# Attention on full 128x128 matmuls, and doubles converted in six VectorE instructions

## The chip, the cores and the metric

One core of a Trainium2 chip runs the whole program. The metric is device time in microseconds (us) from one execution to the next; lower is better. TensorE does matmuls (PE in the rows, its weight loads PEld), VectorE is DVE, ScalarE is ACT, GpSimd is POOL, SyncE (SP) issues most DMAs.

## The reference

Three parts follow one another: attention with a compressive memory (32 heads of 576 queries and 64 dimensions), a mixture of 8 experts where each token takes one, and a dense FFN.

```python
scores = scale * q @ k.T                         # B, H, S, D = 4, 8, 576, 64
scores = where(causal, -1e9, scores)
a = softmax(scores)
local = a @ v
q_p = where(q > 0, q, exp(q) - 1) + 1
mem_out = (q_p @ M_prev) / (q_p @ z_prev + 1e-6)
x = g * mem_out + (1 - g) * local                # to 2304 tokens x 512
...
expert_idx = argmax(normalized(x) @ normalized(expert_emb).T / tau)
out[e] = gate * (relu(x[e] @ w1[e]) @ w2[e])     # 512 -> 1024 -> 512
...
h = x @ w_in                                     # 512 -> 2048 -> 512
return (h * clip(h + 3, 0, 6) / 6) @ w_out
```

The weights of the last part arrive as 64-bit floats' bit patterns (the doubles of the title) and are turned into 32-bit ones on the chip.

## The kernel before

**Attention** runs over 16 pairs of heads. A pair has nine score tiles of 128 queries: t = 0 to 3 of head 0 (y = 0), then t = 4, which holds the last 64 queries of both heads (q4, L212), then t = 0 to 3 of head 1. For each tile, `scores` (L250 on) issues the score matmuls with a mask added by one bf16 matmul (L274, L276), VectorE takes the maximum (L281) and ScalarE the exponential (L287); `turn` transposes the result (L297, L301) and ScalarE copies it to aT (L298, L302); `sumup` multiplies it with the values (L310); `finish` normalizes and adds the memory's part (L315 to L321). The loop runs scores five tiles ahead of `turn` (LA = 5) and `sumup` one behind; three PSUM tiles hold scores, two hold po.

A head has 64 dimensions, so a score matmul contracts over 64 rows. For pairs 1 to 15 the product is made in fp32r from split operands: kx holds the high part of k on the head's own 64 partitions and the low part on the other 64, so that one 128-row matmul of qx (the high part of q on both halves) gives high x (high + low) (L269); a second one, on 64 rows, adds ql, the low part of q (L270). Tile t = 0 of every head, and pair 0 wholly, use fp32 matmuls on 64 rows (L266). A fp32 matmul is two instructions in the trace, a fp32r one is one. The operands are made by `split_pair` (qs on ScalarE L209, kx L220 and L222, qx on VectorE L221, ql on GpSimd L223), nine tiles ahead of the pair's first `turn`, so four ahead of its first score tile; the loads are 18 ahead (`load_pair`).

`mem_pair` makes the memory's part (L228 to L248): five matmuls of 130 columns (L236), the last with a stationary operand of 64 columns. In `sumup`, t = 4 is done twice, once a head, with a stationary operand of 64 columns and, for the last keys, 64 rows (128*64 and 64*64 in the rows). `route_pair` and `route` choose experts; at a batch's end (4 pairs) GpSimd scatters token ids by indirect DMA (L399).

**The experts** run in slots of 256 or 128 tokens, eight steps a slot: weights are split into fp32r high (ScalarE, L726) and low (GpSimd or VectorE, L727), hidden layer in `l1` (L735 to L737), its result split into hh and hl (ScalarE L781, VectorE L782), and down projection (L793 to L795) two steps later, which needs hl. Beside it `piece` converts the dense weights, 32 pieces of 512 elements, by `to_f32`: seven VectorE instructions (L680 to L686) and one on GpSimd (L687).

**The dense FFN** runs last, in nine chunks of 256 tokens.

The order on each engine is a scheduler's: program order where data allow, with operations that are ready earlier moved ahead.

## Time and profile before

| | |
|---|---|
| time, median of 3 runs | 1119.07 us (1113.79 to 1120.48) |
| profiled execution | 1113.76 us, span 1112.1 us |
| mean granted TensorE clock | 0.946 |
| TensorE busy | 1039.5 us (93%), 7214 matmuls |
| VectorE, ScalarE, GpSimd busy | 59%, 43%, 35% |
| DMA | 116.90 MB, mean 105 GB/s |

The span runs from the first to the last instruction of the profiled execution. Matmuls are pipelined, so the time that one takes off the span is the distance from its start to the next one's start; the listed duration also holds what overlaps the neighbour. A row's stretch shows stages that the mean over the span hides.

### The profile page before, as it was taken

The numbers are of one execution on the slowest core, as the hardware profiler recorded it, in microseconds if no ns is written. First come the engines' busy times: TensorE is split into PE (matmuls) and PEld (weight loads), VectorE is DVE, ScalarE is ACT, GpSimd is POOL, SyncE is SP. The second block draws the span as 40 slices with busy tenths as digits, with TensorE's granted clock in tenths as the row PEclk, the third lists the DMA queues.
The fourth block names the chain that finished last, engine by engine and source line by source line (L and its number), as shares of the span: only waits on it lengthen the run. The fifth ranks groups of instructions, "written<-read, shape, count | busy, mean of one in ns | idle before, by whom it ended". The sixth has DMA issues, their size and how long they took to land. (4 is left out here: it accounts for less than half of the span.)

```text
span 1112.1 us, 19567 instructions
## 1 busy us (share of the span) xinstructions
PE 1039.5 (93%) x7214; PEld 924.5 (83%) x7214; DVE 651.5 (59%) x1548; ACT 479.6 (43%) x997; POOL 390.7 (35%) x320
## 2 busy tenths in 40 slices
PE   8999899999998888978888889999999999999996
PEld 6778678788778888978887888898989999999895
DVE  5777556645767868688788877732333333333332
ACT  5766445536554444244144425432333333333332
POOL 4444424333545557476376643540000000000000
PEclk9999769959999999899988989999999999999998
DMA  9443924633326965675676555002000000000000
GB/s 215 109 114 90 137 71 101 105 96 89 34 59 245 198 200 188 223 253 198 224 240 225 191 198 213 3 2 21 20 1 19 20 1 20 10 10 20 1 19 20
DMA packets 89655, 116.90 MB, mean 105 GB/s; under 512 B 54856, under 2 KB 59336, under 8 KB 89552
## 3 DMA queue, kind: packets, MB, share of 16 engines
q1 hardware_dynamic: 85072, 105.08, 35.1%
q0 software_dynamic: 4480, 10.51, 2.5%
q8 instruction: 58, 0.95, 0.4%
q14 instruction: 45, 0.37, 0.1%
HBM read 105.64 MB, written 9.91 MB: 104 GB/s over the span
## 5 line engine op out<-in xcount | busy, mean ns | idle before, releaser
L1007 DVE SCALAR_TENSOR_TENSOR t<-t,ph 128x256 f32<-128x256 f32 x144 | 60.5, 420 | 168.4 <-ACT t L1005 166.9
L737 PE MATMUL ph<-xl,hw 128*128 128x256 f32 x468 | 136.3, 291 | 7.9 <-DVE xl L746 7.9
L727 POOL TENSOR_TENSOR lw<-rw,hw 128x1024 fp32r<-128x1024 f32 x50 | 126.1, 2530 | 43.1 <-ACT hw L726 29.5
L977 POOL DMA_INDIRECT out<-ob,pmt x18 | 17.3, 960 | 341.9 <-DVE ob L1023 306.0
L1005 ACT ACTIVATE t<-ph,half 128x256 f32<-128x256 f32 x144 | 68.4, 475 | 159.8 <-PE ph L737 159.0
L736 PE MATMUL ph<-xh,lo 128*128 128x256 f32 x480 | 134.1, 279 | 0.0
L735 PE MATMUL ph<-xh,hw 128*128 128x256 f32 x448 | 131.6, 294 | 0.2 <-ACT xh L745 0.2
L310 PE MATMUL po<-vt,aT 128*128 128x65 f32 (+2 forms) x960 | 127.3, 268 | 4.0 <-ACT aT L298 2.5
L310 PEld LDWEIGHTS po<-vt,aT 128*128 128x128 f32 (+2 forms) x960 | 116.4, 187 | 13.5 <-issue 5.5
L795 PE MATMUL py<-hl,hw 128*128 128x256 f32 x288 | 88.3, 307 | 37.2 <-DVE hl L782 36.0
L726 ACT CAST hw<-rw 128x1024 fp32r<-128x1024 f32 x72 | 75.5, 1050 | 109.1 <-PE py L795 85.5
L281 DVE TENSOR_REDUCE nmx<-ps 128x1 f32<-128x256 f32 (+4 forms) x160 | 74.8, 477 | 68.8 <-PE ps L274 40.2
L298 ACT COPY aT<-ptr 128x128 f32<-128x128 f32 (+2 forms) x144 | 63.7, 445 | 103.0 <-PE ptr L297 97.8
L988 PE MATMUL po<-lo,gh 128*128 128x512 f32 x270 | 106.9, 396 | 0.0
L737 PEld LDWEIGHTS ph<-xl,hw 128*128 128x128 f32 x468 | 92.9, 198 | 9.3 <-DVE xl L746 9.3
L1011 DVE TENSOR_TENSOR gl<-t,gh 128x256 fp32r<-128x256 f32 x144 | 61.3, 425 | 64.7 <-ACT gh L1010 64.7
L736 PEld LDWEIGHTS ph<-xh,lo 128*128 128x128 f32 x480 | 90.5, 189 | 4.7
L736 PE MATMUL ph<-xh,lw 128*128 128x256 f32 x320 | 94.2, 294 | 0.0
L795 PEld LDWEIGHTS py<-hl,hw 128*128 128x128 f32 x288 | 59.6, 207 | 40.5 <-DVE hl L782 38.9
L1010 ACT CAST gh<-t 128x256 fp32r<-128x256 f32 x144 | 58.5, 406 | 77.2 <-DVE t L1007 77.2
L687 POOL TENSOR_TENSOR x<-f,u 128x512 int32<-128x512 int32 x32 | 56.8, 1775 | 98.9 <-DVE f L686 98.9
L735 PEld LDWEIGHTS ph<-xh,hw 128*128 128x128 f32 x448 | 89.6, 200 | 1.5 <-ACT xh L745 0.4
(299 smaller groups left out, 2772.0 us busy)
## 6 DMA issues: line engine op xcount, KB each, us to landing
rw<-in_wm SPq DMA_DIRECT2D x92, 512.0 KB, 3.9
raw<-in_w SPq DMA_DIRECT2D x32, 512.0 KB, 5.7
k<-in_kT SPq DMA_DIRECT2D x30, 256.0 KB, 5.0
q<-in_qT SPq DMA_DIRECT2D x30, 192.0 KB, 5.0
kp<-in_kT SPq DMA_DIRECT2D x16, 288.0 KB, 3.0
qp<-in_qT SPq DMA_DIRECT2D x16, 288.0 KB, 4.1
vt<-in_v SPq DMA_DIRECT2D x32, 128.0 KB, 4.9
xg<-xb SPq DMA_DIRECT2D x16, 256.0 KB, 5.3
```

The lines of the kernel that those rows point to most:

```text
L281: nc.vector.tensor_reduce(nmx[:, k:k + 1], ps, AX.X, ALU.max, negate=True)
L298: ev(aT[:, :nf].rearrange("p j r -> p (j r)"), ptr[:, :nf * P])
L310: nc.tensor.matmul(po[:r, t, :], aT[:kn, j, c:c + r], vt[:kn, y, j, :], start=(j == 0), stop=(j == t))
L726: st["copy"] = nc.scalar.copy(hi, raw)
L727: st["split"] = eng.tensor_tensor(lo, raw, hi.bitcast(F32), ALU.subtract)
L735: nc.tensor.matmul(ph, a, xh, start=(c == 0), stop=False)
L736: nc.tensor.matmul(ph, b, xh, start=False, stop=False)
L737: nc.tensor.matmul(ph, a, xl, start=False, stop=(c == 3))
L795: nc.tensor.matmul(o, a, hl, start=False, stop=(f == 7 and d % 2 == 1))
L988: nc.tensor.matmul(po[t], a, lo[:, 512:], start=False, stop=False)
L1005: nc.scalar.activation(t6, ph, AF.Relu, bias=half[:, :1], scale=1.0 / 6.0)
L1011: low = nc.vector.tensor_tensor(gl, gg, gh.bitcast(F32), ALU.subtract)
```

## The change

- `sumup` does t = 4 once for both heads: vt is laid out by key tile and then head, so that the values of both heads stand side by side and one full matmul gives 64 queries of either head times 130 columns; the diagonal blocks of the result are used. The last 64 keys lie on partitions 64 to 127 of vt behind 64 rows of zeros, and `turn` transposes the last 128 columns of a.
- `split_pair` loads and splits all 512 queries: q2 is scaled in place by ScalarE, qx is one copy, and ql one subtraction on all 128 partitions. t = 0 of pairs 1 to 15 uses the split operands too, and the ql matmul contracts over 128 rows, which adds low x low.
- `mem_pair` pads ph to five full tiles and copies the result out in two instructions instead of three.
- `finish` of head 0 runs after its fourth tile, and that of head 1 takes the last queries of both heads.
- `to_f32` masks small values by a float maximum instead of a compare and an and.

Pair 0's scores stay on 64 rows.

```diff
@@ -91,28 +91,29 @@
...
-    vt_b = [ac.tile([P, 2, NT, D + 1], F32, name=f"vt{i}", tag=f"vt{i}") for i in range(3)]
+    vt_b = [ac.tile([P, NT, 2, D + 1], F32, name=f"vt{i}", tag=f"vt{i}") for i in range(3)]
     for vt in vt_b:
         nc.vector.memset(vt[:, :, :, D:], 1.0)
+        nc.vector.memset(vt[:64, 4], 0.0)
...
-            q2 = p2.tile([P, 2, KW - P], F32, name="q2", tag="q2")
+            q2 = p2.tile([P, 2, KW], F32, name="q2", tag="q2")
...
-            nc.sync.dma_start(out=q2[o], in_=qflat[h, P:KW].rearrange("(y d) s -> d y s", y=2))
+            nc.sync.dma_start(out=q2[o], in_=qflat[h, :KW].rearrange("(y d) s -> d y s", y=2))
...
         for y in range(2):
-            nc.sync.dma_start(out=vt[:, y, :4, :D], in_=vi[y, :4 * P].rearrange("(c p) d -> p c d", p=P))
-        nc.sync.dma_start(out=vt[:64, :, 4, :D], in_=vi[:, 4 * P:].rearrange("y p d -> p y d"))
+            nc.sync.dma_start(out=vt[:, :4, y, :D], in_=vi[y, :4 * P].rearrange("(c p) d -> p c d", p=P))
+        nc.sync.dma_start(out=vt[64:, 4, :, :D], in_=vi[:, 4 * P:].rearrange("y p d -> p y d"))
@@ -194,51 +198,51 @@
...
-    rs_b = [ac.tile([P, NT], F32, name=f"rs{i}", tag=f"rs{i}") for i in range(2)]
+    rs_b = [ac.tile([P, 4 + i], F32, name=f"rs{i}", tag=f"rs{i}") for i in range(2)]
...
     def split_pair(i, ld):
         kp, qp, k2, q2, vt = ld
-        qs = p2.tile([P, KW], F32, name="qs", tag="qs")
         q4 = q4_b[i % 3]
-        nc.scalar.mul(qs, qp[:, :KW], 0.125)
+        if i == 0:
+            qs = ac.tile([P, KW], F32, name="qs", tag="qs")
+            nc.scalar.mul(qs, qp[:, :KW], 0.125)
+        else:
+            nc.scalar.mul(q2, q2, 0.125)
         for y in range(2):
             r = slice(64 * y, 64 * y + 64)
             nc.vector.tensor_scalar(q4[r, 64 * y:64 * y + 64], qp[r, KW:], 0.125, None, ALU.mult)
         if i == 0:
             return kp, qs, q4, None, None, None, vt
         kx = p2.tile([P, 2, KW], F32R, name="kx", tag="kx")
-        qx = p2.tile([P, 2, KW - P], F32R, name="qx", tag="qx")
-        ql = p2.tile([P, KW - P], F32R, name="ql", tag="ql")
+        qx = p2.tile([P, 2, KW], F32R, name="qx", tag="qx")
+        ql = p2.tile([P, 2, KW], F32R, name="ql", tag="ql")
+        nc.vector.tensor_copy(qx, q2)
         for y in range(2):
-            r, o = slice(64 * y, 64 * y + 64), slice(64 - 64 * y, P - 64 * y)
+            o = slice(64 - 64 * y, P - 64 * y)
             (nc.scalar.copy if y else nc.vector.tensor_copy)(kx[:, y], k2[:, y])
-            nc.vector.tensor_scalar(qx[:, y], q2[:, y], 0.125, None, ALU.mult)
             nc.gpsimd.tensor_tensor(kx[o, y], k2[o, y], kx[o, y].bitcast(F32), ALU.subtract)
-            nc.gpsimd.tensor_tensor(ql[r], qs[r, P:], qx[r, y].bitcast(F32), ALU.subtract)
-        return kp, qs, q4, kx, qx, ql, vt
+        nc.gpsimd.tensor_tensor(ql, q2, qx.bitcast(F32), ALU.subtract)
+        return kp, None, q4, kx, qx, ql, vt
...
-        ph = p2.tile([P, S], F32, name="ph", tag="ph")
-        nc.scalar.activation(ph, qp, AF.Relu)
...
+        ph = p2.tile([P, NT * P], F32, name="ph", tag="ph")
+        nc.scalar.activation(ph[:, :S], qp, AF.Relu)
+        yield
+        nc.vector.scalar_tensor_tensor(ph[:, :S], ex, 1.0, ph[:, :S], ALU.min, ALU.add)
+        nc.vector.tensor_copy(ph[:, S:], ph[:, 4 * P:S])
         for lo, hi in ((0, 3), (3, 5)):
             pm = ps_m.tile([P, 512], F32, name="pm", tag="pm")
             for t in range(lo, hi):
-                nc.tensor.matmul(pm[:RT[t], (t - lo) * W:(t - lo + 1) * W], ph[:, t * P:t * P + RT[t]],
-                                 mz[:, i, :], start=True, stop=True)
-            n = min(hi, 4) - lo
-            nc.scalar.copy(mem[:, lo:lo + n].rearrange("p t y d -> p (t y d)"), pm[:, :n * W])
-            if hi == 5:
-                nc.scalar.copy(mem[:64, 4].rearrange("p y d -> p (y d)"), pm[:64, n * W:(n + 1) * W])
+                nc.tensor.matmul(pm[:, (t - lo) * W:(t - lo + 1) * W], ph[:, t * P:(t + 1) * P], mz[:, i, :],
+                                 start=True, stop=True)
+            nc.scalar.copy(mem[:, lo:hi].rearrange("p t y d -> p (t y d)"), pm[:, :(hi - lo) * W])
@@ -262,12 +266,11 @@
...
-                if t == 0 or t < 4 and kx is None:
+                if t < 4 and kx is None:
                     nc.tensor.matmul(o, qs[r, c], kp[r, x0:x1], start=True, stop=False)
                 elif t < 4:
-                    c = slice((t - 1) * P, t * P)
                     nc.tensor.matmul(o, qx[:, y, c], kx[:, y, x0:x1], start=True, stop=False)
-                    nc.tensor.matmul(o, ql[r, c], kx[r, y, x0:x1], start=False, stop=False)
+                    nc.tensor.matmul(o, ql[:, y, c], kx[:, y, x0:x1], start=False, stop=False)
@@ -298,28 +301,38 @@
...
-            nc.tensor.transpose(pt2[:64, :P], a[:, 4 * P:], ident)
-            nc.scalar.copy(aT[:64, 4], pt2[:64, :P])
+            nc.tensor.transpose(pt2[:, :P], a[:, S - P:], ident)
+            nc.scalar.copy(aT[:, 4], pt2[:, :P])
         return aT
 
     def sumup(t, aT, vt, po, y):
-        r = RT[t]
-        c = 64 * y if t == 4 else 0
+
         for j in range(t + 1):
-            kn = RT[j]
-            nc.tensor.matmul(po[:r, t, :], aT[:kn, j, c:c + r], vt[:kn, y, j, :], start=(j == 0), stop=(j == t))
+            o, w = po[:, t * D1:(t + 1) * D1], vt[:, j, y, :]
+            if t == 4:
+                o, w = po[:, 4 * D1:], vt[:, j].rearrange("p y d -> p (y d)")
+            nc.tensor.matmul(o, aT[:, j, :], w, start=(j == 0), stop=(j == t))
...
     def finish(i, y, po, mem, xb):
         h = (2 * i + y) % H
         rs = rs_b[y]
-        nc.vector.tensor_scalar(rs[:, :4], po[:, :4, D], 1e-9, None, ALU.add)
-        nc.vector.tensor_scalar(rs[:64, 4:5], po[:64, 4, D:], 1e-9, None, ALU.add)
+        o = po[:, :4 * D1].rearrange("p (t d) -> p t d", d=D1)
+        nc.vector.tensor_scalar(rs[:, :4], o[:, :, D], 1e-9, None, ALU.add)
+        if y:
+            for z in range(2):
+                r, e = slice(64 * z, 64 * z + 64), (5 + z) * D1
+                nc.vector.tensor_scalar(rs[r, 4:5], po[r, e - 1:e], 1e-9, None, ALU.add)
         nc.vector.reciprocal(rs, rs)
-        nc.vector.tensor_scalar(rs, rs, omg[:, h:h + 1], None, ALU.mult)
-        for t in range(NT):
-            r = RT[t]
-            nc.vector.scalar_tensor_tensor(xb[:r, t, h * D:(h + 1) * D], po[:r, t, :D], rs[:r, t:t + 1],
-                                           mem[:r, t, y, :D], ALU.mult, ALU.add)
+        nc.vector.tensor_scalar(rs[:, :4], rs[:, :4], omg[:, h:h + 1], None, ALU.mult)
+        for t in range(4):
+            nc.vector.scalar_tensor_tensor(xb[:, t, h * D:(h + 1) * D], o[:, t, :D], rs[:, t:t + 1],
+                                           mem[:, t, y, :D], ALU.mult, ALU.add)
+        if y:
+            nc.vector.tensor_tensor(rs[:, 4:5], rs[:, 4:5], omg4[:, h // 2:h // 2 + 1], ALU.mult)
+            for z in range(2):
+                r, e = slice(64 * z, 64 * z + 64), (4 + z) * D1
+                nc.vector.scalar_tensor_tensor(xb[:64, 4, (h - 1 + z) * D:(h + z) * D], po[r, e:e + D],
+                                               rs[r, 4:5], mem[r, 4, z, :D], ALU.mult, ALU.add)
@@ -609,11 +622,9 @@
...
             if u == 0 or u == 4:
-                pos[j, u > 0] = ps_o.tile([P, NT, D + 1], F32, name="po", tag="po")
-            for yy in ((y,) if t < 4 else (0, 1)):
-                sumup(t, aTs[m], sp[j][-1], pos[j, yy], yy)
-            aTs.pop(m)
-            if u == 4 or u == 8:
+                pos[j, u > 0] = ps_o.tile([P, 6 * (D + 1)], F32, name="po", tag="po")
+            sumup(t, aTs.pop(m), sp[j][-1], pos[j, u >= 4], y)
+            if u == 3 or u == 8:
                 finish(j, y, pos.pop((j, y)), mem_b[j % 2], xb_b[bj % 2])
@@ -670,20 +681,19 @@
 
 def to_f32(nc, cv, src, dst, n):
...
-    m = cv.tile([P, n], I32, name="m", tag="m", bufs=1)
-    v.tensor_scalar(f, hi, 4, 1, ALU.logical_shift_left, ALU.logical_shift_right)
-    v.tensor_scalar(m, hi, 1, None, ALU.logical_shift_left)
+    v.tensor_scalar(f, hi, 1, 1, ALU.logical_shift_left, ALU.logical_shift_right)
+    v.tensor_scalar(f.bitcast(F32), f.bitcast(F32), 2.0 ** -15, None, ALU.max)
     v.tensor_scalar(u, lo, 28, 1, ALU.logical_shift_right, ALU.bitwise_and)
-    v.scalar_tensor_tensor(f, lo, 29, f, ALU.logical_shift_right, ALU.bitwise_xor)
-    v.tensor_scalar(m, m.bitcast(mybir.dt.uint32), float(897 << 21), -1.0, ALU.is_ge, ALU.mult)
-    v.scalar_tensor_tensor(f, f, 0x40000000, m, ALU.bitwise_xor, ALU.bitwise_and)
-    v.scalar_tensor_tensor(f, hi, -0x80000000, f, ALU.bitwise_and, ALU.bitwise_or)
+    v.tensor_scalar(f, f, 3, 0x3fffffff, ALU.logical_shift_left, ALU.bitwise_and)
+    v.scalar_tensor_tensor(f, lo, 29, f, ALU.logical_shift_right, ALU.bitwise_or)
+    v.scalar_tensor_tensor(f, hi, -0x40000000, f, ALU.bitwise_and, ALU.bitwise_or)
     return nc.gpsimd.tensor_tensor(dst, f, u, ALU.add)
```

## Rows read from the trace of the kernel before

**Rows 1.** Stretches: length, busy us (count) PE, PEld, DVE, ACT, POOL; granted clock, DMA.

```profile
15.00:125.00 110.00, 108.05 (x801) 84.74 (x799) 79.46 (x258) 71.43 (x168) 49.87 (x42) 1.00 0.57 111
125.00:156.00 31.00, 28.46 (x118) 21.86 (x119) 13.94 (x44) 10.88 (x27) 8.29 (x7) 0.51 0.57 131
217.00:248.00 31.00, 30.79 (x129) 24.39 (x130) 15.70 (x47) 12.36 (x30) 11.85 (x10) 0.51 0.42 100
352.00:695.00 343.00, 293.66 (x2287) 287.50 (x2286) 272.26 (x421) 136.24 (x219) 193.80 (x102) 0.94 0.66 214
```

**Rows 2.** The same columns, ahead of the second stretch at a lower clock.

```profile
214.70:217.60 2.90, 0.66 (x6) 0.47 (x6) 1.08 (x5) 1.03 (x3) 0.00 (x0) 1.00 0.75 45
```

**Rows 3.** The page's costliest groups: busy us, mean ns, idle us before, releaser.

```profile
L795 PE MATMUL py<-hl,hw 128*128 128x256 f32 x288 | 88.3, 307 | 37.2 <-DVE hl L782 36.0
```

**Rows 4.** Timeline of TensorE: start us, duration us. A 512-column score tile.

```profile
164.64 0.48 PE L269 MATMUL ps<-kx,qx 128*128 128x512 f32 x1
165.06 0.50 PE L270 MATMUL ps<-kx,ql 64*128 64x512 f32 x1
165.49 0.23 PE L274 MATMUL ps<-negm,identb 128*128 128x128 bf16 x1
```

**Rows 5.** Timeline of TensorE: L269 ahead of a full fp32 instruction.

```profile
173.56 0.48 PE L269 MATMUL ps<-kx,qx 128*128 128x512 f32 x1
173.88 0.51 PE L342 MATMUL plg<-enT,xT 128*128 128x8 f32 x4
```

**Rows 6.** Timeline of TensorE in the expert stage: full fp32r instructions.

```profile
505.16 0.28 PE L737 MATMUL ph<-xl,hw 128*128 128x256 f32 x1
505.28 0.28 PE L793 MATMUL py<-hh,hw 128*128 128x256 f32 x1
```

**Rows 7.** Timeline of TensorE: t = 0 of pairs 1 and 2.

```profile
20.72 0.48 PE L266 MATMUL ps<-kp,qs 64*128 64x128 f32 x2
21.14 0.23 PE L274 MATMUL ps<-negm,identb 128*128 128x128 bf16 x1
...
39.20 0.48 PE L266 MATMUL ps<-kp,qs 64*128 64x128 f32 x2
```

**Rows 8.** Timeline of TensorE: full fp32 instructions of 65 and 130 columns.

```profile
177.06 0.78 PE L310 MATMUL po<-vt,aT 128*128 128x65 f32 x6
177.67 0.89 PE L236 MATMUL pm<-mz,ph 128*128 128x130 f32 x6
178.40 0.27 PE L297 MATMUL ptr<-ident,a 128*128 128x128 f32 x1
```

**Rows 9.** Timeline of TensorE: the sums of t = 4, and what follows.

```profile
169.81 1.80 PE L310 MATMUL po<-vt,aT 128*64 128x65 f32 x20
171.54 0.83 PE L342 MATMUL plg<-enT,xT 128*128 128x8 f32 x6
```

**Rows 10.** Timeline of TensorE at the lower clock.

```profile
225.00 0.79 PE L270 MATMUL ps<-kx,ql 64*128 64x512 f32 x1
225.73 0.29 PE L274 MATMUL ps<-negm,identb 128*128 128x128 bf16 x1
```

**Rows 11.** Timeline of GpSimd: ql of pairs 1 and 2.

```profile
25.13 2.59 POOL L223 TENSOR_TENSOR ql<-qs,qx 64x384 fp32r<-64x384 f32 x2 [0.30 <-DVE qx L221]
...
40.58 2.05 POOL L223 TENSOR_TENSOR ql<-qs,qx 64x384 fp32r<-64x384 f32 x2
```

**Rows 12.** Timeline of GpSimd in the expert stage: lw subtractions.

```profile
524.48 5.07 POOL L727 TENSOR_TENSOR lw<-rw,hw 128x1024 fp32r<-128x1024 f32 x2
```

**Rows 13.** Timeline of GpSimd after a batch's scatter: idle before kx.

```profile
220.14 1.27 POOL L222 TENSOR_TENSOR kx<-k,kx 64x512 fp32r<-64x512 f32 x1 [11.25 <-DMA ids<-tok,idp]
```

**Rows 14.** One line each: duration ns min/median/max, first and last start.

```profile
L684 DVE TENSOR_SCALAR m<-m x32: 410/414/2622, 414.4 to 690.2; 128x512 int32<-128x512 uint32 x32
...
L685 DVE SCALAR_TENSOR_TENSOR f<-f,m x32: 672/682/3196, 415.1 to 691.7; 128x512 int32<-128x512 int32 x32
```

**Rows 15.** Timeline of VectorE in the expert stage.

```profile
524.73 2.62 DVE L681 TENSOR_SCALAR m<-raw 128x512 int32<-128x512 int32 x1
```

More of the change, by code (lines that the diff above doesn't have):

```diff
@@ L163, in attention @@
     omg = ac.tile([P, H], F32, name="omg", tag="omg")
+    omg4 = ac.tile([P, H // 2], F32, name="omg4", tag="omg4")
     nc.scalar.activation(gb, gb, AF.Exp, scale=-1.0)
@@ L168, in attention @@
         nc.vector.tensor_scalar(omg, gb, -1.0, 1.0, ALU.mult, ALU.add)
+        nc.vector.tensor_copy(omg4[:64], omg[:64, 0::2])
+        nc.vector.tensor_copy(omg4[64:], omg[64:, 1::2])
     enT = r1.tile([P, 4, E], F32, name="enT", tag="enT")
@@ L196, in attention @@
     q4_b = [ac.tile([P, P], F32, name=f"q4{i}", tag=f"q4{i}") for i in range(3)]
-    rs_b = [ac.tile([P, NT], F32, name=f"rs{i}", tag=f"rs{i}") for i in range(2)]
+    rs_b = [ac.tile([P, 4 + i], F32, name=f"rs{i}", tag=f"rs{i}") for i in range(2)]
+    D1 = D + 1
     for q4 in q4_b:
@@ L200, in attention @@
     for i in range(2):
-        nc.vector.memset(mem_b[i], 1.0)
-        nc.vector.memset(rs_b[i], 1.0)
         nc.gpsimd.memset(xb_b[i][64:, NT - 1, :], 0.0)
@@ L228, in mem_pair @@
         nc.scalar.activation(ex, qp, AF.Exp)
-        ph = p2.tile([P, S], F32, name="ph", tag="ph")
-        nc.scalar.activation(ph, qp, AF.Relu)
+        ph = p2.tile([P, NT * P], F32, name="ph", tag="ph")
+        nc.scalar.activation(ph[:, :S], qp, AF.Relu)
         yield
-        nc.vector.scalar_tensor_tensor(ph, ex, 1.0, ph, ALU.min, ALU.add)
+        nc.vector.scalar_tensor_tensor(ph[:, :S], ex, 1.0, ph[:, :S], ALU.min, ALU.add)
+        nc.vector.tensor_copy(ph[:, S:], ph[:, 4 * P:S])
         for lo, hi in ((0, 3), (3, 5)):
```

## The prediction

> **What bounds the kernel now.** I read the table of stretches first, because three stages with different limits share one span. Attention (15 to 345 us) has TensorE busy 108 of 110 us [rows 1]; VectorE is busy 72% there (79.46 of 110), ScalarE 65%, GpSimd 45%. So TensorE's issue order sets the time, and a price of this stage is the distance from one matmul's start to the next one's, not its listed duration, which overlaps its neighbour. In two stretches of 31 us (125 to 156, 217 to 248) the granted clock is 0.51, that is 1.2 instead of 2.4 GHz. TensorE completes 118 and 129 matmuls there, 3.8 and 4.2 per us against 801/110 = 7.3 elsewhere: work for 16 and 18 us, so each stretch costs about 14 us. Ahead of the second, for 2.9 us, TensorE was busy 0.66 us, VectorE 1.08, ScalarE 1.03 and GpSimd 0 [rows 2]. In the expert stage (352 to 695) TensorE is busy 293.66 of 343 us and VectorE 272.26 [rows 1]: VectorE comes late. The group table says for whom: the third matmul of the down projection sat idle 37.2 us, 36.0 of it for hl on VectorE [rows 3]. The last stage, the dense FFN, is not touched by the diff.
>
> **Score matmuls of pairs 1 to 15 (30 heads, t = 1 to 3).** One timeline of TensorE gives the 512-column tile: L269 starts at 164.64, L270 (64 rows) at 165.06, the mask L274 at 165.49 [rows 4]. That is 0.42 + 0.43 = 0.85 us. L269 followed by another 128-row instruction instead takes 173.88 - 173.56 = 0.32 [rows 5], so 0.10 of the 0.42 is the change of shape. The after form, a full 128x128 fp32r matmul behind another, has a row in the expert stage: 256 columns every 0.12 us [rows 6], hence 0.24 for 512. The new L269 to L270 is that form, 0.24. The new L270 to L274 (fp32r, then bf16, both full) has no row: below it lies 0.24, above it 0.32 (fp32r, then fp32); I take the middle, 0.28. So 0.85 becomes 0.52, a gain of 0.33 (0.29 to 0.37). What is lost is mostly the two changes of shape, which don't depend on the width, so I give the 256 and 384 tiles the same: 90 pairs x 0.33 = 29.7 us (26 to 33).
>
> **The same at t = 0.** Two fp32 64-row instructions take 20.72 to 21.14 = 0.42 [rows 7], and one change of shape ahead of them 0.10: 0.52. They become two fp32r ones on 128 columns. Lower bound: half of the 256-column distance, 0.06 each; upper: the 0.10 of a full fp32 one, (177.67 - 177.06)/6 [rows 8]. I take 0.20 for both: 30 x 0.32 = 9.6 us (9 to 12).
>
> **Last queries' sums.** Twenty narrow instructions run from 169.81 to 171.54 = 1.73 us [rows 9]; with the change of shape ahead of them, 0.10, it is 1.83. Ten full ones of 130 columns replace them; L236 has that form, six from 177.67 to 178.40 = 0.12 each [rows 8]: 1.2. Gain 0.63 x 16 = 10.1 us (9 to 11). Half of each product is thrown away; the doubled width is free only because 65 and 130 columns cost 0.10 and 0.12.
>
> **mem's last tile.** Two narrow instructions between two changes of shape become full ones: 2 x 0.10, 16 times: 3.2 us (2 to 4). The padding copy (64 columns, VectorE) and the wider evacuation on ScalarE, which replaces two, lie under TensorE.
>
> These add to 52.6 us at 2.4 GHz. About 4 heads of 30 fall into the 1.2 GHz stretches, where the 64-row instruction of 512 columns takes 225.73 - 225.00 = 0.73 instead of 0.43 [rows 10], 1.7 times: 4/30 x 52.6 x 0.7 = 4.9. **Attention loses 57 us of TensorE's issue time** (50 to 62).
>
> A rule speaks against this part. The Trainium skill, "TensorEngine Tiling (Array Packing)", section Key Properties, says that tiles run in parallel, and its section Theoretical Speedup promises up to 2x for a contraction of 64 rows or fewer. The rows show none of it here: the 64-row L270 takes 0.43 between two 128-row instructions, where a full one takes 0.24 [rows 4, 6]. By the rule L270 would be free now and cost something afterwards; the rival below prices that.
>
> **What the edit asks of other engines.** Per pair: ScalarE scales 1024 columns of q2 instead of 512 of qp; VectorE copies qx in one instruction instead of two; GpSimd makes ql in one instruction of 1024 columns on 128 partitions instead of two of 384 on 64. GpSimd took 2.59 us for the two, 768 columns [rows 11]; by columns that is 3.5 us for the new one, and by its subtractions of 1024 columns, two in 5.07 us, 2.5 [rows 12]. It now follows both kx subtractions. The two q2 loads grow by a third, on the same SyncE queue in the same places. finish of head 0 moves one tile earlier and issues no DMA; VectorE's count in it goes from 18 to 19 a pair. All this has TensorE as cover: VectorE's 72% would become 72% x 330/(330 - 57 + 12) = 83%. Without that cover the longer ql alone would cost up to 3.5 - 2.6 = 0.9 us a pair, 13 us.
>
> **The added wait.** t = 0 of pairs 1 to 15 used qs and kp; now it needs kx, qx and ql, one tile (about 2 us) sooner than before. TensorE queues the transposes and sums of five older tiles around it, and behind those stand VectorE's maxima and ScalarE's exponentials. Pair 1: t = 0 ran at 20.72, ql ended at 25.13 + 2.59 = 27.72 [rows 7, 11]. That is 7.0 us late; older tiles' sums can be ordered ahead and fill some of it, I take 5. Pair 2: 39.20 against 40.58 + 2.05 = 42.63, 3.4 late: I take 2. At a batch's end GpSimd was held 11.25 us behind its scatter before kx [rows 13], and a TensorE that is 15% faster meets that sooner: 2 us at two batches. With 1 for the rest: 12 us (3 to 30; below, nearly all hidden; above, 2 us at each of 15 pairs).
>
> **Doubles.** Seven VectorE instructions of 512 elements become six, 32 times. Shifts read 0.414 us at the median on contiguous data (L684), two-source ones 0.682 (L685) [rows 14]. Before: four and three of them; after: four (max and the shift-and counted as L684) and two. One two-source instruction goes, 0.68 us, 22 us in all on VectorE. Of that only what stands ahead of a late hl counts. A larger part of the lateness is no instruction count: L681 took 2.62 us instead of 0.41 while GpSimd ran two lw subtractions (5.07 us) [rows 15, 12]. The order after the edit still puts single-source instructions there, so these waits stay. Bounds: 0 (hl ahead of the instruction that goes) and 22 (all of it); I take 8 us, a dozen of the 32.
>
> **The sum.** 57 - 12 + 8 = 53 us. Span 1112.1 - 53 = 1059.1; 1.7 us lie around it (1113.76): 1060.8. That execution is the fastest end of the runs (1113.79 to 1120.48), their median 5.3 higher; I add half, **1064 us**.
>
> **Rivals.**
> - *The clock.* If one or both 1.2 GHz stretches of attention go, it is 14 or 28 us less: 1036 to 1050. For it: TensorE fell after stalls in which all engines were nearly idle [rows 2], and other timing may avoid one. Against: the scatter that GpSimd waits for stays. 0.20.
> - *New waits eat half.* ql late by 2 us at most pairs, or VectorE at 83% with two-port instructions behind a longer ql: 30 us instead of 12, and the doubles give nothing: 1064 + 18 + 8 = 1090. 0.18. For it: pair 1's lateness [rows 7, 11]; against: 11.25 us of delay before kx [rows 13] did not keep TensorE from staying busy in 217 to 248 [rows 1].
> - *Conversion order turns worse.* One more instruction of each of the 11 slots behind GpSimd (11 x 2.6 us, [rows 15]): +29, 1093. 0.05.
> - *Slower.* ql late at every pair. Gains of 57 + 8 are used up at 4.3 us a pair, and over 1% slower needs 5.1 us x 15: about 1125. Only pair 1 shows a lateness of that size. 0.03.
> - *64-row matmuls do overlap.* Then no issue time comes off the scores, and 30 x (0.12 + 0.18 + 0.24) = 16 us are added, against 13 for sums and mem and 8 for the doubles: 1109, no change. The rows speak plainly against it: 0.02. This is what the Trainium skill's page named above would make of it.
>
> **How the numbers follow.** The forecast with the clock as it was, 1050 to 1080, has 0.51; the rivals' stand behind them, and 0.01 is left for no change at all. A range of 1036 to 1093 holds forecast, clock, half-eaten gain and most of the worse order; it leaves out 0.06 and the edges of the others. Faster by over 1% (below 1107.9): 0.51 + 0.20 + 0.18 + 0.05 = 0.94; within 1%, about what a measurement of this kernel can tell from none: 0.03; slower by over 1%: 0.03.
>
> **What would show it.** L269 to L270 at 512 columns 0.24 and L270 to L274 0.28 in the new timeline; ten L310 instructions in 1.2 us; attention's end near 300 instead of 345; a wait for ql near 22 to 28 us; VectorE above 80% in attention; idle before the down projection's third matmul near 29 us. Wrong would be: L270 still above 0.4, or a table of waits headed by TensorE behind ql at many pairs.

## The result

The changed kernel runs in 1085.9 us at the median of four runs (1081.77 to 1089.39), the kernel before, beside it, in 1119.78 (1113.79 to 1125.89). The ratio is 0.9696, with a 95% interval from 0.9630 to 0.9761: 3% faster, where 1064 us (5%) was forecast. 1085.9 lies inside the forecast range. The rival that stood nearest is "new waits eat half", with 1090 us. Every ratio in this document leaves out the slow runs of both kernels (those over 1.5% above the fastest), while a median holds all runs, so a ratio need not be the quotient of two medians.

The profiled execution of after took 1088.07 us, with a span of 1086.4, that of before 1113.76 with 1112.1; so the two traces show 25.7 us of difference where the medians show 34. TensorE's table of stretches, before and then after, for attention (15 us to the first expert matmul) and for the expert stage (length, then busy us and count of PE, PEld, DVE, ACT, POOL; clock, DMA share, GB/s):

```profile
15.00:342.00 327.00, 319.98 (x2194) 254.44 (x2192) 210.80 (x747) 187.42 (x442) 136.11 (x114) 0.90 0.48 103
342.00:701.00 359.00, 306.26 (x2389) 299.70 (x2389) 285.80 (x442) 144.75 (x231) 208.00 (x107) 0.94 0.65 209
```

```profile
15.00:332.00 317.00, 276.68 (x2045) 246.24 (x2045) 224.52 (x768) 191.70 (x428) 139.73 (x99) 0.90 0.57 110
332.00:677.00 345.00, 302.00 (x2392) 295.30 (x2392) 262.27 (x409) 145.72 (x233) 204.40 (x107) 0.96 0.66 220
```

Attention became 10 us shorter (327 to 317), not 45. TensorE's busy time there fell by 43.3 us (319.98 to 276.68), but its idle time, length less busy, rose from 7.0 to 40.3. So most of what the matmuls gave up came back as waits. The mean clock is 0.90 in both. The expert stage became 14 us shorter (359 to 345), where 8 were forecast; the row of after that answers [rows 3] in the page's table of costliest groups has 27.5 us of idle time instead of 37.2:

```profile
L805 PE MATMUL py<-hl,hw 128*128 128x256 f32 x288 | 85.4, 297 | 27.5 <-DVE hl L792 27.5
```

TensorE's timeline after, at the full clock: a 512-column score tile and a t = 0 tile (answering [rows 4, 7]), then the last queries' sums with what follows (answering [rows 9]); start us, duration us.

```profile
170.83 0.48 PE L272 MATMUL ps<-kx,qx 128*128 128x512 f32 x1
171.15 0.40 PE L273 MATMUL ps<-kx,ql 128*128 128x512 f32 x1
171.38 0.23 PE L277 MATMUL ps<-negm,identb 128*128 128x128 bf16 x1
...
175.41 0.30 PE L272 MATMUL ps<-kx,qx 128*128 128x128 f32 x1
175.55 0.28 PE L273 MATMUL ps<-kx,ql 128*128 128x128 f32 x1
175.67 0.23 PE L277 MATMUL ps<-negm,identb 128*128 128x128 bf16 x1
```

```profile
24.17 1.28 PE L314 MATMUL po<-vt,aT 128*128 128x130 f32 x10
25.29 0.38 PE L300 MATMUL ptr<-ident,a 128*128 128x128 f32 x2
```

The two score matmuls of 512 columns take 0.32 + 0.23 = 0.55 us from start to start instead of 0.85; those of t = 0 take 0.14 + 0.12 = 0.26; the ten sums take 1.12. All three moved the way that was forecast, the first two by less. The new thing is TensorE's table of waits over attention (total us, times, longest):

```profile
PE po L314 <- ACT aT L301: 13.9, 3, 11.4
PE ps L275 <- ACT a L290: 8.2, 3, 3.2
PE ps L273 <- POOL ql L229: 4.3, 3, 1.8
PE pm L243 <- ACT mem L245: 4.3, 5, 1.8
PE prk L396 <- DVE ohb L392: 2.8, 1, 2.8
```

The kernel before had 7.0 us in four such rows, the longest wait 2.4 us. After, ql itself is behind 4.3 us only. The rest waits for ScalarE (transposed scores, exponentials, copies of mem) and VectorE, and one single wait is 11.4 us long.

### The profile page after: what moved, and what is told of

Read it like the earlier page. It is cut to its first block, busy times and chain, and to the rows that moved or that the text cites. A ratio compares the mean times of both kernels' runs of the same rounds, so it can differ in the third digit from the quotient of the medians.

```text
span 1086.4 us, 19212 instructions
## 1 busy us (share of the span) xinstructions
PE 990.2 (91%) x7054; PEld 911.0 (84%) x7054; DVE 639.8 (59%) x1534; ACT 483.1 (44%) x981; POOL 388.5 (36%) x305
## 5 line engine op out<-in xcount | busy, mean ns | idle before, releaser
L314 PE MATMUL po<-vt,aT 128*128 128x65 f32 (+1 forms) x800 | 119.6, 285 | 13.9 <-ACT aT L301 13.9
L314 PEld LDWEIGHTS po<-vt,aT 128*128 128x128 f32 x800 | 113.3, 209 | 16.8 <-ACT aT L301 15.8
L736 ACT CAST hw<-rw 128x1024 fp32r<-128x1024 f32 x72 | 75.3, 1050 | 100.5 <-PE py L805 69.0
L805 PE MATMUL py<-hl,hw 128*128 128x256 f32 x288 | 85.4, 297 | 27.5 <-DVE hl L792 27.5
L290 ACT ACTIVATE a<-ps,nmx 128x256 f32<-128x256 f32 (+4 forms) x160 | 82.1, 529 | 34.1 <-DVE nmx L284 23.9
L803 PE MATMUL py<-hh,hw 128*128 128x256 f32 x288 | 83.6, 290 | 0.0
## 6 DMA issues: line engine op xcount, KB each, us to landing
xg<-xb SPq DMA_DIRECT2D x16, 256.0 KB, 10.7
```

The costliest lines, as they stand in the source:

```text
L290: nc.scalar.activation(a[:, x0:x1], ps, AF.Exp, bias=nmx[:, k:k + 1])
L314: nc.tensor.matmul(o, aT[:, j, :], w, start=(j == 0), stop=(j == t))
L736: st["copy"] = nc.scalar.copy(hi, raw)
L803: nc.tensor.matmul(o, a, hh, start=(f == 0 and d % 2 == 0), stop=False)
L805: nc.tensor.matmul(o, a, hl, start=False, stop=(f == 7 and d % 2 == 1))
```

## The experiments

Each kernel has its ratio to the kernel before, run beside it on the same chip: that kernel's median was 1128.57 us for e1 to e4, 1124.22 for e5, e6, e7 and e9, and 1125.26 for e8, e10, e11 and e12, so ratios are compared, not times. The columns on attention come from a table of stretches of each trace, as above; TensorE's idle time is the length less its busy time.

| kernel | median us | ratio (95%) | attention us | PE busy | PE idle | clock |
|---|---|---|---|---|---|---|
| before | | 1 | 327 | 320.0 | 7.0 | 0.90 |
| after | 1085.90 | 0.9696 (0.9630 to 0.9761) | 317 | 276.7 | 40.3 | 0.90 |
| e1, doubles only | 1109.14 | 0.9891 (0.9843 to 0.9938) | 335 | 322.7 | 12.3 | 0.89 |
| e2, attention only | 1105.13 | 0.9888 (0.9839 to 0.9937) | 317 | 282.2 | 34.8 | 0.88 |
| e3, before without the scatter | 1079.08 | 0.9668 (0.9591 to 0.9745) | 293 | 291.8 | 1.2 | 1.00 |
| e4, after without the scatter | 1052.64 | 0.9424 (0.9359 to 0.9489) | 279 | 257.3 | 21.7 | 0.98 |
| e5, q2 scaled by VectorE | 1092.78 | 0.9695 (0.9647 to 0.9743) | 323 | 286.2 | 36.8 | 0.88 |
| e6, finish after t = 4 | 1085.42 | 0.9624 (0.9571 to 0.9678) | 307 | 272.0 | 35.0 | 0.92 |
| e7, ql on 64 rows | 1121.76 | 1.0006 (0.9959 to 1.0053) | 342 | 320.5 | 21.5 | 0.86 |
| e8, t = 0 on 64 rows | 1084.87 | 0.9599 (0.9514 to 0.9684) | 308 | 275.0 | 33.0 | 0.91 |
| e9, ql in four | 1066.70 | 0.9488 (0.9443 to 0.9534) | 293 | 263.2 | 29.8 | 0.94 |
| e10, e9 and e6 together | 1066.96 | 0.9473 (0.9413 to 0.9532) | 297 | 267.7 | 29.3 | 0.91 |
| e11, e10 and earlier loads | 1061.82 | 0.9445 (0.9380 to 0.9510) | 291 | 264.4 | 26.6 | 0.93 |
| e12, after again | 1091.96 | 0.9686 (0.9617 to 0.9756) | 322 | 277.1 | 44.9 | 0.89 |

Traces of the same code differ too. The attention of before takes 327 us in its own trace and 335 in e1; that of after takes 317, 317 and 322 us in after, e2 and e12, with 40.3, 34.8 and 44.9 us of idle time. Smaller differences than these between two traces are no evidence by themselves.

**The two halves of the change.** e1 is the kernel before with the new `to_f32` alone; e2 is the changed kernel with the old one.

> The kernel before with the six-instruction conversion alone. If the 14 us that the expert stage lost belong to the conversion: 1105 us (1100 to 1110), attention as before, idle before the third matmul of the down projection near 28 us instead of 37. If they came from attention ending earlier and other timing of the slots: 1116 to 1120 us.

> The kernel after with the seven-instruction conversion of before. If the two parts add: 1085.9 + 14 = 1100 us, and the attention stage about 317 us long. If the parts help each other (shorter stalls keep the clock up): above 1105 us.

Each half is worth 1.1%, and 0.9891 x 0.9888 = 0.978, where both together have 0.9696. The product lies just outside the interval of 0.9630 to 0.9761, but each of its factors is uncertain by 0.5% itself, so whether the halves help each other isn't settled. The doubles do it where they should: the idle time ahead of the third down-projection matmul is 23.1 us in e1 and stays 37.8 in e2 (table of groups of e1, then of e2).

```profile
L794 PE MATMUL py<-hl,hw 128*128 128x256 f32 x288 | 85.4, 297 | 23.1 <-DVE hl L781 21.7 <-issue 1.4
```

```profile
L806 PE MATMUL py<-hl,hw 128*128 128x256 f32 x288 | 87.5, 304 | 37.8 <-DVE hl L793 37.4 <-DVE lw L738 0.4
```

So the doubles gave what was forecast, and more; what is missing is missing from attention, which was to give 45 us and gave some 12.

**Is it the scatter of token ids?** After a batch, GpSimd scatters ids to memory, and TensorE's 11.4-us wait lies there. e3 and e4 are the kernels before and after without that scatter; the experts of both then gather token 0 throughout.

```diff
-            nc.gpsimd.indirect_dma_start(ids_d[t][:], bass.IndirectOffsetOnAxis(ap=idp[:r, t:t + 1], axis=0),
-                                         tok[:r, b, t:t + 1], None)
```

> The kernel before without the scatter of token ids (L399 left out; the experts then gather token 0 everywhere, and the time is to be read with that). My theory: the stalls of 1.6 + 2.6 + 2.4 us of attention go, and with them the two stretches of 31 us at the lower clock (28 us): about 1085 us. If the clock falls without those stalls too: 1112 us.

> The kernel after without the scatter of token ids (left out as in the run above). My theory: of the 38 us in which TensorE waited in attention, those near the scatters go (about 25 us), and the short stretches at the lower clock with some of them: 1050 us (1045 to 1060), 35 us or more below the other one without scatter if that one keeps its clock low, about the same 35 if both run at the full clock. Rival, VectorE's load is what TensorE waits for: not below 1075 us, and waits in attention still above 30 us.

The scatter is dear to both kernels, but it isn't the main thing that ate the gain. Without it the change is worth 0.9424/0.9668 = 0.975, 2.5%, no more than the 3.0% with it, and the times lie 26 us apart, where the theory wanted 35 or more. Attention of e3, and then of e4 (columns as above):

```profile
15.00:308.00 293.00, 291.84 (x2194) 232.91 (x2193) 209.12 (x748) 187.64 (x442) 122.02 (x99) 1.00 0.47 114
```

```profile
15.00:294.00 279.00, 257.26 (x2041) 227.70 (x2040) 230.64 (x771) 191.50 (x427) 125.68 (x85) 0.98 0.52 123
```

Without the scatter, the attention of before has a full clock and 1.2 us of idle time: it is bound by TensorE and nothing else, and both of its stretches at the lower clock [rows 1] had come from the scatter's stalls. TensorE's work shrinks by 34.6 us between the two rows, and 20.6 of them return as idle time that no scatter causes. With the scatter in place the idle time rose by 33.3 us (7.0 to 40.3); so some 20.6 of these belong to the change alone, and some 12.7 to a scatter that costs the faster kernel more.

**Does q2's scaling stand in ScalarE's way?** This is the 11.4-us wait, on ScalarE and on TensorE (start, duration, idle before and its releaser):

```profile
227.80 1.06 ACT L215 ACTIVATE q<-q 128x1024 f32<-128x1024 f32 x1 [11.85 <-DMA q<-in_qT]
228.77 0.46 ACT L301 COPY aT<-ptr 128x384 f32<-128x384 f32 x1
```

```profile
229.28 1.54 PE L314 MATMUL po<-vt,aT 128*128 128x65 f32 x6 [11.40 <-ACT aT L301]
```

ScalarE stood in its queue at q2's load, with the copies of transposed scores behind it, while the scatter was under way. The table of DMA from 202 to 220 us, in 40 equal slices of 0.45 us, shows what the load met:

```profile
GB/s 396 369 123 14 5 5 14 0 0 0 9 27 14 27 14 28 23 18 0 55 18 59 41 269 315 168 0 5 36 14 9 18 0 14 18 9 18 0 5 50
```

Within two slices the rate falls from 369 GB/s to 14, and apart from three slices it doesn't come back. In e4, without the scatter, ScalarE doesn't wait for q2's load in any pair. e5 lets VectorE scale q2, which takes that load out of ScalarE's queue.

```diff
-            nc.scalar.mul(q2, q2, 0.125)
+            nc.vector.tensor_scalar(q2, q2, 0.125, None, ALU.mult)
```

> The kernel after with q2 scaled by VectorE instead of ScalarE. Theory A, the wait of 11.6 us at 217.6 belongs to ScalarE standing in its queue before a late load of q2: it goes, 1076 us (1073 to 1080). Rival: VectorE, which has 0.7 us a pair more to do, stands before the same load, and the maxima behind it: 1086 us or up to 1094, with the wait at the same place under VectorE's name.

The long wait is gone (the longest one left is 3.6 us), but the ratio is 0.9695, that of the changed kernel, and TensorE's idle time is 36.8 us. VectorE has 238 us of work in attention instead of 225, and the waits are many and short. Taking the longest wait away bought nothing that can be measured. The rival did not come either: VectorE never waits for q2's load in this trace. That VectorE had no room for the 13 us of scaling is likely, and isn't shown; nor is it shown that e5's edit removed the wait, since it is missing from the traces of e8 and e10 too, where ScalarE still scales q2.

**Is finish too early?**

```diff
-            if u == 3 or u == 8:
+            if u == 4 or u == 8:
```

> The kernel after with finish of head 0 behind t = 4 again, as before the change. If moving it one tile earlier made VectorE stand before GpSimd's product for mem (4.0 us twice, TensorE 3.1 and 3.0 us at its t = 4 tiles): 1080 us (1077 to 1083). If mem comes so late that it stands there one tile later too: 1084 to 1088.

The ratio is 0.9624 against 0.9696; the intervals overlap, so a gain of 0.7% isn't settled. VectorE's wait for GpSimd's product (mem), 8.0 us in after and 4.0 at the longest, is 4.7 and 2.4 us here; it got shorter and did not go.

**Is the shape of the ql matmul the gain?** e7 contracts over 64 rows again and keeps the rest of the change.

```diff
-                    nc.tensor.matmul(o, ql[:, y, c], kx[:, y, x0:x1], start=False, stop=False)
+                    nc.tensor.matmul(o, ql[r, y, c], kx[r, y, x0:x1], start=False, stop=False)
```

> The kernel after with the ql matmul on 64 rows again (low x low left out as before), all else as after. If TensorE's issue time sets attention, 120 tiles with two changes of shape at 0.10 and 0.19 us: 1086 + 30 = 1116 us (1108 to 1120). If waits for other engines set it, they swallow most of it: 1092 us (1088 to 1098), with waits in attention down from 38 to 15 us.

A 384-column tile of e7 at the full clock, from TensorE's timeline:

```profile
195.93 0.42 PE L272 MATMUL ps<-kx,qx 128*128 128x384 f32 x1
196.28 0.44 PE L273 MATMUL ps<-kx,ql 64*128 64x384 f32 x1
196.65 0.23 PE L277 MATMUL ps<-negm,identb 128*128 128x128 bf16 x1
```

That is 0.35 + 0.37 = 0.72 us from the first start to the mask's. Over the trace the medians at 256, 384 and 512 columns are 0.606, 0.724 and 0.835 us, those of before to within 3 ns, where after has 0.325, 0.438 and 0.552; at t = 0 it is 0.49 instead of 0.26. Over 30 heads this one line costs 32 us of issue time. The whole gain is gone (1.0006), the doubles' share too. That is more than the attention half gave (1.1%): the line is back for t = 0 as well, which before did in another form, and the stage's clock is 0.86 instead of 0.90, so that TensorE's busy time of 320.5 us against 276.7 is in part the clock's.

The Trainium skill, "TensorEngine Tiling (Array Packing)", section Key Properties, which the prediction set against this part, says that different tiles can work in parallel, but also that changing the tiling mode drains TensorE. The trace agrees with the second: a 64-row matmul between two 128-row ones costs more than a full one, 0.37 us to the next start against 0.18 at 384 columns, and the one ahead of it 0.35 against 0.26.

**Is the long ql instruction the cause of the waits?** The new ql is one GpSimd instruction of 1024 columns. One pair of the changed kernel, first GpSimd and VectorE, then ScalarE, then TensorE:

```profile
89.14 2.36 POOL L229 TENSOR_TENSOR ql<-q,qx 128x1024 fp32r<-128x1024 f32 x1 [0.68 <-DMA k<-in_kT]
```

```profile
89.66 2.46 DVE L238 SCALAR_TENSOR_TENSOR ph<-ex,ph 128x576 f32<-128x576 f32 x1
92.04 0.14 DVE L288 TENSOR_TENSOR nmx<-nmx 128x1 f32<-128x1 f32 x1
```

```profile
92.22 0.53 ACT L290 ACTIVATE a<-ps,nmx 128x320 f32<-128x320 f32 x1 [2.23 <-DVE nmx L288]
92.64 0.48 ACT L245 COPY mem<-pm 128x390 f32<-128x390 f32 x1
```

```profile
93.17 0.71 PE L243 MATMUL pm<-mz,ph 128*128 128x130 f32 x4 [1.77 <-ACT mem L245]
```

ql runs from 89.14 to 91.50. VectorE's two-source instruction L238 begins within it and takes 2.46 us, where its line's median is 0.752; it ends 0.62 us behind ql. Behind it stand the maximum (L288), for which ScalarE's exponential waits 2.23 us, behind that the copy of mem, and for that TensorE waits 1.77 us. That GpSimd's and VectorE's paths to memory are shared, and that VectorE instructions with two inputs contend for them, is what the Trainium skill states in "GPSIMD Engine Reference", section Specifications, which names instructions in a two-port mode beside them; the rows agree for L238, and give the size: until the GpSimd instruction ends. Copies and casts with one source were held in the same way (L392, a cast of 40 columns, for 2.37 us, median 0.18). e9 makes ql in four instructions of 256 columns.

```diff
-        nc.gpsimd.tensor_tensor(ql, q2, qx.bitcast(F32), ALU.subtract)
+        for y in range(2):
+            for c in (slice(0, 256), slice(256, KW)):
+                nc.gpsimd.tensor_tensor(ql[:, y, c], q2[:, y, c], qx[:, y, c].bitcast(F32), ALU.subtract)
```

> The kernel after with ql made by four GpSimd instructions of 256 columns instead of one of 1024 (0.5 us more of GpSimd's time a pair). Theory B, VectorE's two-port instructions stand behind the long one (ph 2.46 us instead of 0.75, ohb 2.37 instead of 0.17): the waits after them go, 1077 us (1073 to 1081), and the longest L238 falls below 1.6 us. Rival: what TensorE waits for comes from scatters and loads alone: 1084 to 1090.

0.9488 against 0.9696: 2.1% for two lines, although GpSimd now spends 60 x 0.727 = 43.6 us on ql instead of 15 x 2.362 = 35.4. The same place of the same pair, GpSimd, VectorE and TensorE:

```profile
81.81 3.29 POOL L231 TENSOR_TENSOR ql<-q,qx 128x256 fp32r<-128x256 f32 x4 [0.68 <-DVE qx L224]
```

```profile
82.00 1.15 DVE L240 SCALAR_TENSOR_TENSOR ph<-ex,ph 128x576 f32<-128x576 f32 x1
```

```profile
85.43 0.71 PE L245 MATMUL pm<-mz,ph 128*128 128x130 f32 x4 [1.03 <-ACT mem L247]
```

VectorE's instruction gets through after the first part, in 1.15 us. Over the trace that line's longest instruction is 1.469 us instead of 2.686. Two limits of this reading: VectorE's instructions are held for hardly less time in sum, mainly for less at once (its busy time in attention is 220.7 us, from 224.5); and the first part of ql is also ready earlier, so that TensorE's waits for ql fall from 4.3 to 2.1 us. The runs don't part these two effects; that GpSimd's narrower instructions are worth 2% is shown, and the share of each way isn't. Nor is the gain idle time alone: of the 24 us that attention is shorter (317 to 293), 10.5 are TensorE's idle time and 13.5 its busy time, for as many matmuls (2045 and 2047), at a mean clock of 0.94 instead of 0.90. In e10, which has the same four parts, it is 11.0 and 9.0. So about half of the gain came through the clock, which fell for less of the time.

**Do these gains add, and what of the scatter?** e12 is the changed kernel again, for a comparison on the same chip. e10 has ql in four and the late finish. e11 also loads k, q, k2 and q2 five tiles earlier than the values. (The four parts have 256 columns each, also where an expectation gives other widths.)

```diff
...
-        for at, act in ((AT_LOAD, load), (AT_SPLIT, split), (AT_MEM, mem)):
+        for at, act in ((AT_LOAD - 5, load), (AT_LOAD, values), (AT_SPLIT, split), (AT_MEM, mem)):
```

> The changed kernel once more, beside the next three on one chip, so that they can be read against it and not only against the kernel before. Ratio to the kernel before 0.970 as in its first comparison (0.963 to 0.976). If this ratio comes out below 0.96, the 2% that the narrower GpSimd subtractions seemed to give was the chip's, and not theirs.

> The changed kernel with ql made in four subtractions of 256 and 128 columns, and with the finish of the first head after t = 4 again. Theory (one 2.35-us GpSimd subtraction holds VectorE's work on two reads, and the finish of the last tile is itself late in a full VectorE): the two gains, 2.1% and 0.7%, lie at different tiles and add, so the ratio is 0.942 against 0.970 of the changed kernel. Rival: both only relieve the same full VectorE at the same tiles; then the ratio is that of the narrower subtractions alone, 0.949, or worse.

> As the one with ql in four and the late finish, and k, q and their half-width copies k2 and q2 are loaded five tiles earlier than the values, so that the scatter of the token ids does not find them under way. Theory (the scatter stops the loads that the next pair's split waits for): the 8 to 9 us for which TensorE stands at the scatter go, and most of the low clock after it, some 8 to 12 us in all: ratio 0.933. Rival: what stands is not the load but something behind it on ScalarE or VectorE that waits for the scatter in another way; then the ratio stays at that of the kernel without the early loads.

e12 repeats the changed kernel's ratio, 0.9686, so the 2% of the four parts is not the chip's. e10 is at 0.9473, where e9 alone was at 0.9488: the late finish adds nothing that can be measured, and the rival's figure (0.949) fits better than the theory's 0.942. e11 is at 0.9445, the best ratio of all that computes the whole result, 1061.82 us; from e10 it can't be told apart. In its trace a wait at the scatter is still there, 6.6 us long, now behind GpSimd, whose kx waited 11.27 us. First TensorE and GpSimd of e11, then GpSimd of after:

```profile
208.61 0.47 PE L279 MATMUL ps<-kx,qx 128*128 128x128 f32 x1 [6.62 <-POOL kx L233]
```

```profile
207.30 1.26 POOL L233 TENSOR_TENSOR kx<-k,kx 64x512 fp32r<-64x512 f32 x1 [11.27 <-DMA vt<-in_v]
```

```profile
227.13 1.26 POOL L228 TENSOR_TENSOR kx<-k,kx 64x512 fp32r<-64x512 f32 x1 [13.06 <-DMA ids<-tok,idp]
```

The load that the row of e11 names can't be what released kx: kx doesn't read vt, and that load landed at 207.35, after kx had begun. The last of the batch's scatters landed at 207.0. In after, the row names the scatter itself (ids), as [rows 13] did for before. So GpSimd most likely stands until its own scatter has landed, whatever the loads do, which is close to the rival; why kx waits for it isn't shown. Loading five tiles earlier doesn't get the work past the scatter; the theory's 0.933 lies outside the interval.

**What did t = 0 give?** e8 puts the first tile's scores back on 64 rows in fp32, from 128 columns of q that ScalarE scales for it.

```diff
...
-                if t < 4 and kx is None:
+                if t == 0 or t < 4 and kx is None:
```

> The changed kernel with the first query tile's scores of each pair back in fp32 on 64 rows, from columns scaled by ScalarE. The prediction put the change of this part at 9.6 us less issue for TensorE. With the durations that the trace of after shows (0.142 and 0.116 us for the two matmuls of 128 columns in place of two that took 0.11 and more each) theory: the issue time rises by only some 4 us, the ql that a pair's first tile had to wait for is now first needed two tiles later, and the ratio stays within 0.5% of the changed kernel's. Rival (the forecast's sizes hold): 9 to 10 us slower, ratio 0.979.

Its ratio is 0.9599 and that of e12 beside it 0.9686; the intervals overlap. It isn't slower, as the rival had it. TensorE's issue time (reckoned as in the next section) is longer than in e12, 260.6 us against 251.8; but that leans on kinds of neighbours that come only a few times, and with each kind's median taken over all traces it is 255.0 against 250.2. So the run doesn't decide between the forecast's 9.6 and my 4. Whatever t = 0 earned in issue time does not show in the kernel's time. The likely reason is that it comes back as waits: TensorE's idle time is 33.0 us in e8, 40.3 in after and 44.9 in e12. But it is 34.8 in e2, which has the attention of after, and the wait at the scatter varies between traces of one code (11.4 us in after, 13.7 in e12; in e8 it came as two of 6 us). So that isn't settled.

## Why the prediction was right in direction and too large

The direction held, and so did the mechanism of the gain: the shape of the score matmuls is its core (e7), and each of its terms moved the way it was said to. The size did not hold: 34 us instead of 55 by the medians. 1085.9 lies outside the 1050 to 1080 of the forecast itself, which had 0.51; the stated range held because it took in the rivals. Two terms were mis-sized, issue time and waits.

**Issue time: 52.6 us forecast, 40 measured.** To compare terms I added up the distances from each matmul's start to the next one's over attention, taking for every kind of neighbours the median at the full clock times their count. That gives 292.8 us before and 252.7 after; other ways to count rare kinds move these figures by some 2 us. What lies above it, and isn't the lower clock, is waits: 6.1 us before and 38.3 after; the lower clock adds 27.9 and 25.8. By this account all scores together gave 78.6 - 51.9 = 26.7 us where 29.7 + 9.6 = 39.3 were forecast. The sums gave 10.7 (10.1 forecast) and mem 3.9 (3.2). The transposes of xb gave 2.9, not forecast, and some 4 were lost in other rows, where short waits may be counted as issue.

The step that failed here is the one that took 0.24 us for L269's successor from [rows 6], a matmul that follows another fp32r one. L272 follows fp32 work, and that costs. The prediction's own [rows 5] had 0.32 for L269 ahead of a full instruction, which is what came. The trace of before also had a row with both cases, in the expert stage:

```profile
506.83 0.93 PE L756 MATMUL px<-ident,xr 128*128 128x128 f32 x7
507.51 0.36 PE L735 MATMUL ph<-xh,hw 128*128 128x256 f32 x1
507.72 0.28 PE L736 MATMUL ph<-xh,lw 128*128 128x256 f32 x1
507.83 0.28 PE L737 MATMUL ph<-xl,hw 128*128 128x256 f32 x1
```

The first L735 after fp32 transposes takes 0.21 us to the next start, its follower 0.11; over the trace, L735 has a median of 0.20 behind fp32 transposes and of 0.12 behind fp32r matmuls. So the new L272 to L273 is 0.32, not 0.24, while L273 to L277 is 0.23, a little under the 0.28 taken. The gain of a tile is 0.28 to 0.29 us at each of the three widths (medians of 0.837 to 0.552, 0.724 to 0.438, 0.608 to 0.325), so giving all widths the same was right. That makes 25.6 us at 90 pairs rather than 29.7. At t = 0 the two new matmuls take 0.26 us and not 0.20. The rest probably lies in what stands around them: a change of shape ahead of the matmul is booked on its predecessor, and in 18 of the 90 tiles of before other work stood between L269 and L270 anyway.

**Waits: 12 us forecast, 32 measured** (6.1 to 38.3; by length less busy, 33.3). The prediction looked for them at ql's own lateness, with pair 1 at its head; there the forecast was ample, as all waits for ql come to 4.3 us. Its sentence that the other engines' work "has TensorE as cover" is the step that failed here. It counted the cover as a share of busy time: 83% forecast for VectorE over the stage. Measured it is 224.52/317 = 71% over the stage (64% before), and by that number nothing should wait. But each tile runs in a chain, scores, maximum, exponential, transpose, copy, sums, with a buffer of a few tiles in between, and one VectorE instruction held for 2.4 us stops the chain however idle VectorE is in the mean (the pair at 89 us, and e9). That was in the rival's words, "two-port instructions behind a longer ql", which got 0.18: a right mechanism, whose 30 us of waits came, priced together with a failure of the doubles that did not come. That its 1090 us lie so near is luck in part: the issue time that fell short took the place of the doubles. Of the 33.3 us by which idle time rose, 12.7 go with the scatter (e3, e4) and 10.5 with the long ql instruction (e9). If the two add, which no run shows, some 10 us stay open, about as much as idle time differs between traces of one code.

In before, an instruction of the same VectorE line took up to 1.65 us, and TensorE lost hardly anything by it: it was the slowest engine. That 14% less work of its own (276.68 us for 319.98) is what laid the other waits open is argued, not shown; the longer hold is part of it.

**Doubles: 8 us forecast, 14 measured** (expert stage 359 to 345; 0.9891 alone, 12 us). VectorE's busy time in the stage fell by 285.80 - 262.27 = 23.5 us, near the 22 forecast. The forecast's 8 us were late hl, and that part came nearly as said: TensorE's idle time in the stage fell by 9.7 us (359 - 306.26 = 52.7 to 345 - 302.00 = 43.0), as much as the idle time ahead of the third matmul of the down projection (37.2 to 27.5). The other 4.3 us are TensorE's busy time for the same matmuls, at a clock of 0.96 instead of 0.94, which the forecast did not count. The conversion order's rival did not come.

**The clock.** Attention's mean clock is 0.90 in both traces, as the forecast assumed. The two stretches of 31 us became a dozen of 3 to 14 us, as long in sum: 217 to 248 us has 0.78 now instead of 0.51 [rows 1]. e3 shows what the rival was worth: 1.00 all through attention, and 34 us.

**64-row overlap** fell with e7. Two rivals' times, 1109 and 1125, leave out the half of 5.3 us that the forecast adds, and 1125 is less than 1% above 1119.07.

**The tells:** ten sums in 1.2 us (1.12) and a wait for ql near 28 us (1.30 at 30.98) came; attention's end near 300 us (331.8), VectorE above 80% and 0.24 for the first score matmul did not; the idle time before the down projection's third matmul came to 27.5 (29 said). The sum: 40 of issue and 2 at the lower clock, less 32 of waits, plus 14 in the expert stage and 1.7 after it, is the 25.7 us between the spans.

## What to carry to other kernels

When one engine is busy 98% of a stage, the others' mean load says little about what happens once it gets faster: look in the timeline for their longest single instructions and for what stands behind each, because the faster engine may meet that next. Price a matmul by the distance to the next start behind the same kind of predecessor, shape and type, not behind its own like. Count what fewer stalls give back through the clock, too. And an instruction on an engine off the path should be cut as short as its consumers allow when it holds another engine up: here four short GpSimd instructions, 8 us longer in sum, were worth 2.1%.

## What the runs showed of the hardware

- One GpSimd subtraction of 2.36 us held a VectorE instruction with two sources for 2.46 us (median 0.75), and another a 40-column cast with one source for 2.37 us (L392, median 0.18).
- While a batch's scatters of 4-byte ids were under way, the core's DMA fell from 369 GB/s to 14 and stayed under 60 for most of 18 us; ScalarE stood 11.85 us at a load, and without the scatter at none. Leaving the scatter out is worth 3.3% of the kernel before; attention went from 327 to 293 us, 5.8 us of it idle time and the rest at a clock of 1.00 instead of 0.90.
- The first fp32r matmul behind fp32 ones costs some 0.08 us more to the next start (medians of 0.20 against 0.12 at 256 columns).
- A 64-row fp32r matmul between full ones costs more than a full one that does twice the work: 0.43 us against 0.23 at 512 columns.
- Stalls of a few us in TensorE's work cost a second time through the clock: the narrower ql instructions took 10.5 us off TensorE's idle time in attention and 13.5 off its busy time, with the mean granted clock at 0.94 instead of 0.90.
